# Attention and a gated MLP on one core: the first unit's gate product on ScalarE and GpSimd, and three moves in the order of work around it

## The chip, the cores and the metric

The kernel runs on one core of a Trainium2 chip. The metric is the device time of one execution in microseconds (us); lower is better. The time before is the median of three runs, 710.67 us (710.22 to 710.93).

## The reference

Causal attention over 4 batches, 12 heads, 448 positions and head size 64, then a gated MLP over the 1792 tokens, all in fp32:

```python
scores = scale * np.matmul(q, k.transpose(0, 1, 3, 2))
scores = np.where(mask, -1000000000.0, scores)
...
attn = attn / (np.sum(attn, axis=-1, keepdims=True) + 1e-09)
x = (attn @ v).transpose(0, 2, 1, 3).reshape(B * S, H * D)      # 1792 x 768
gate = 1.0 / (1.0 + np.exp(-(x @ w_gate)))                      # 768 x 1536
val = x @ w_val
return (gate * val @ w_out).astype(np.float32)                  # 1536 x 768
```

## The kernel before

The work is cut by batch. Attention of a batch handles six pairs of heads; the MLP of a batch is a "unit" of 36 weight pieces (24 for gate and value, 12 for the output), each 128x768 and each used by 18 matmuls of 448 columns. Attention of batch 0 runs alone: this is the **opening**. Then unit 0 runs interleaved with attention of batch 1, unit 1 with batch 2, unit 2 with batch 3, and unit 3 alone. The stretch of unit 0 with batch 1 is called **the first unit** below.

*Attention, batches 0 and 1.* For each pair, TensorE (PE) makes scores in four blocks of 112 rows (tile `s`, L266); VectorE (DVE) masks and takes the minimum (L279, tiles `sm`, `mn`); ScalarE (ACT) takes the exponential (L283); DVE makes the reciprocal of the sums (`r`, L290 and L291); GpSimd (POOL) scales the eight blocks with it (L302); PE transposes them in five groups of four (`trans`, tile `t` of two buffers, L315); each group is copied to `pt` by ACT (L324) or DVE (L326), as the table `EV` says, whose first index is the batch; PE multiplies with the values (L339, 16 matmuls, PSUM tile `m` of three buffers); ACT and DVE split the result into a high and a low part, `xh` (L347) and `xl` (L348).

*A weight piece* (`weight`, L531 on) arrives in unit 0 as 64-bit floats: SyncE's queue loads it (L542, tile `room`), ACT rescales the high words (L545, `wd`), DVE builds the fp32 word from them in three instructions (L547, L549, L552, tile `wr`), and SyncE writes it to DRAM for later units (L555). Then, in every unit, ACT makes the high part (L560, `wh`) and POOL the low part (L561, `wl = wr - wh`). Each product is three matmuls: `xh,wh`, `xl,wh` and `xh,wl`. In later units the piece comes back from DRAM and DVE has no part in it.

*The gate.* After the six steps of a gate piece ACT takes a tanh (L598, tile `sg` in `gt`). After the value piece DVE makes `(sg + 1) * value` in one instruction, one operand in SBUF and one in PSUM (L604), ACT rounds it to `gh` (L606) and POOL takes the remainder `gl` (L607). There are 12 of these in a unit.

*The order.* Every operation is first recorded in a plan with an engine, a cost and a due time (that of the PE step that needs it, less the costs in between); `order` then walks the engines in modelled time and, on each, takes the ready operation that is due first. The engines run that order strictly, each in its own queue. When PE takes up an attention step among the matmuls is set by `att_steps`: per pair four steps, and a tuple gives each of the five transpose groups its step. `plan.behind` holds the load of a weight piece back until a given pair of the opening has its reciprocal.

Of the kernel before, what the change touches and what calls it, by code (L numbers as in the profile page):

```python
# [11 lines left out]
ACTF = mybir.ActivationFunctionType  # L12
ALU = mybir.AluOpType
PSUM = bass.MemoryType.PSUM

B, H, S, D = 4, 12, 448, 64
# [10 lines left out]
HP = H // 2  # L27
# [1 line left out]
LAG = 1  # L29
WIDE = 2  # L30
WC = 512
EV = ((2, 3), (0, 1, 2, 3, 4), (1, 3, 4), (1, 3, 4))
BUFS = dict(w64=3, wd=2, wr=3, ws=3, sm=4, raw=3, pt=3, gt=5, vr=2, st=3)
LAT, LOOK, SLACK = 0.17, 0.06, 0.2

# [148 lines left out]
def kernel(  # L184
# [7 lines left out]
    nc = tc.nc  # L192
    plan = Plan()
# [8 lines left out]
    dve = lambda n: 0.065 + n / 960  # L202
    act = lambda n, psum=0, acc=0: n / 1200 + (0.05 if psum else 0.093) + 0.093 * acc
# [4 lines left out]
    pairs = [dict(b=n // HP, k=n % HP) for n in range(B * HP)]  # L208
# [276 lines left out]
    def att_steps(b):  # L485

        L = []
        for m in range(HP + LAG + 1):
            n, c, d = (b * HP + e if 0 <= e < HP else None for e in (m, m - LAG, m - LAG - 1))
            if n is not None:  # L490
                L.append((0, lambda due, n=n: load(n)))
            if c is not None:
                L.append((0, lambda due, c=c: load_v(c)))
            if b >= WIDE:
                if c is not None:
                    L.append((0, lambda due, c=c: shift(c)))
                one, two = [], []
                if n is not None:
                    for bl, tag in ((0, 1), "s"), ((2,), "t"):
                        one.append((sum(keys(i) / 600 for i in bl) + 0.2, lambda due, n=n, bl=bl, tag=tag: wscore(n, bl, tag, due)))  # L500
                if d is not None:
                    two.append((2.0, lambda due, d=d: wpv(d, due)))
                if n is not None:
                    two.append((0.9, lambda due, n=n: wscore(n, (3,), "s", due)))
                for mine in (one, two):
                    if mine:
                        L.append((sum(w for w, _ in mine), lambda due, mine=mine: together(due, *(f for _, f in mine)), 1.0))
                    else:
                        L.append((0, lambda due: None, 1.0))
                continue  # L510
            steps = []
            if d is not None:
                steps.append((0 if b == 0 else 2, 2.2, lambda due, d=d: pv(d, due)))
            for e in range(5):
                if n is not None and e < 3:
                    bl = ((0, 1), (2,), (3,))[e]
                    steps.append(((0, 1, 2)[e], qk_cost(bl), lambda due, n=n, bl=bl: score(n, bl, due)))
                if c is not None:
                    steps.append(((1, 1, 2, 2, 3)[e], 0.41, lambda due, c=c, e=e: trans(c, e, due)))
            if b == 0:  # L520
                for _, w, f in steps:
                    L.append((w, lambda due, f=f: together(due, f)))
                continue
            for g in range(4):
                mine = [(w, f) for o, w, f in steps if o == g]
                if mine:
                    L.append((sum(w for w, _ in mine), lambda due, mine=mine: together(due, *(f for _, f in mine))))
        return L


    def weight(p):  # L531

        t = new("wr", [128, KD, 128], F32, BUFS["wr"])
        wd = wdram[p % NP]
        if p < NP:
            q = part(2 * DM, BUFS["w64"], p)
            words = lambda: q.t.bitcast(I32).rearrange("p (n t) -> p n t", t=2)
            d = new("wd", [128, KD * 128], I32, BUFS["wd"])
            lo, hi = (lambda: words()[:, :, 0]), (lambda: words()[:, :, 1])
            ri = lambda: t.t.rearrange("p k m -> p (k m)").bitcast(I32)  # L540
            n = KD * 128
            o = plan.op("SP", dma(128 * n * 8), lambda: nc.sync.dma_start(  # L542
                out=q.t.bitcast(I32), in_=wp[p]), [], [(q,)], extra=2.0)
            plan.behind(o, pairs[(1, 2, HP - 1)[min(p, 2)]]["r"].ops[0])
            plan.op("ACT", act(n) + 0.1, lambda: nc.scalar.activation(  # L545
                out=d.t.bitcast(F32), in_=hi().bitcast(F32), func=ACTF.Copy, scale=REBIAS), [(q,)], [(d,)])
            plan.op("DVE", 0.95, lambda: nc.vector.tensor_single_scalar(  # L547
                out=ri(), in_=d.t, scalar=3, op=ALU.logical_shift_left), [(d,)], [(t,)])
            plan.op("DVE", 1.3, lambda: nc.vector.scalar_tensor_tensor(  # L549
                out=ri(), in0=lo(), scalar=29, in1=ri(), op0=ALU.logical_shift_right, op1=ALU.bitwise_or),  # L550
                [(q,)], [(t,)])
            plan.op("DVE", 1.4, lambda: nc.vector.scalar_tensor_tensor(  # L552
                out=ri(), in0=d.t, scalar=-0x80000000, in1=ri(), op0=ALU.bitwise_and, op1=ALU.bitwise_or),
                [(d,)], [(t,)])
            plan.op("SP", dma(128 * n * 4), lambda: nc.sync.dma_start(out=wd.t, in_=t.t), [(t,)], [(wd,)], extra=2.0)  # L555
        else:
            plan.op("SP", dma(128 * KD * 128 * 4), lambda: nc.sync.dma_start(out=t.t, in_=wd.t), [(wd,)], [(t,)], extra=2.0)
        hi_ = new("wh", [128, KD, 128], F32R, BUFS["ws"])
        lo_ = new("wl", [128, KD, 128], F32R, BUFS["ws"])
        plan.op("ACT", act(768), lambda: nc.scalar.copy(hi_.t, t.t), [(t,)], [(hi_,)])  # L560
        plan.op("PL", 2.0, lambda: nc.gpsimd.tensor_tensor(  # L561
            out=lo_.t, in0=t.t, in1=hi_.t.bitcast(F32), op=ALU.subtract), [(t,), (hi_,)], [(lo_,)])
        return hi_, lo_


    def unit_items(u):
# [15 lines left out]
        def f_in(jj, gv, k, due):  # L582
# [8 lines left out]
            ps = st["ps"]  # L591
# [4 lines left out]
            if gv == 0:  # L596
                st["sg"] = sg = new("gt", [128, S], F32, BUFS["gt"])
                plan.op("ACT", act(S, 1), lambda: nc.scalar.activation(  # L598
                    out=sg.t, in_=ps.t[:, :S], func=ACTF.Tanh, scale=0.5), [(ps,)], [(sg,)])
                return  # L600
            sg = st["sg"]
            gg = new("gt", [128, S], F32, BUFS["gt"])
            gh, gl = st["gh"][jj], st["gl"]
            plan.op("DVE", dve(S), lambda: nc.vector.scalar_tensor_tensor(  # L604
                out=gg.t, in0=sg.t, scalar=1.0, in1=ps.t[:, :S], op0=ALU.add, op1=ALU.mult), [(sg,), (ps,)], [(gg,)])
            plan.op("ACT", act(S), lambda: nc.scalar.copy(gh.t, gg.t), [(gg,)], [(gh,)])  # L606
            plan.op("PL", 1.3, lambda: nc.gpsimd.tensor_tensor(  # L607
                out=gl.t[:, jj], in0=gg.t, in1=gh.t.bitcast(F32), op=ALU.subtract), [(gg,), (gh,)], [(gl, jj)])
# [108 lines left out]
```

## Time and profile before

| | |
|---|---|
| median of 3 runs | 710.67 us |
| the profiled execution | 710.71 us |
| its span, first to last instruction | 709.0 us |
| PE busy in the span | 686.1 us (97%) |
| POOL, ACT, DVE busy | 429.1, 335.5, 331.0 us |

The profile is of one execution. Its span lies 1.7 us under the execution's own time. Busy time is by engine; an instruction that waits for a resource after it has begun counts as busy, so a mean duration well over that of the same instruction elsewhere is a wait inside it. PE matmuls are pipelined, and each row's time covers its own pipeline, so rows overlap. "Idle before" is the time in which an engine did nothing before an instruction, with what released it. PEclk is the granted TensorE clock, 1.00 at 2.4 GHz and 0.50 at 1.2 GHz.

### The profile page before, as it was taken

How to read it: one execution, taken by the hardware profiler on the slowest of the kernel's cores; microseconds unless marked ns; L12 is line 12 of the kernel's file. 1: busy time of each engine (PE TensorE's matmuls, PEld its weight loads, DVE VectorE, ACT ScalarE, POOL GpSimd, SP SyncE). 2: the span in 40 equal slices, each digit the busy share in tenths (PEclk: the TensorE clock that was granted, in tenths of full speed). 3: DMA queues.
4: the chain of work that ended last, by engine and by line, in shares of the span. 5: the costliest groups of instructions: out<-in, count | busy, mean ns of one | idle time of the engine just before them, and what ended most of it. 6: DMA issues, size and time to landing. Idle time of an engine off the chain costs nothing.

```text
span 709.0 us, 11071 instructions
## 1 busy us (share of the span) xinstructions
PE 686.1 (97%) x3888; PEld 573.3 (81%) x3888; DVE 331.0 (47%) x778; ACT 335.5 (47%) x727; POOL 429.1 (61%) x388
## 2 busy tenths in 40 slices
PE   7899999989998999999999999999999999999997
PEld 4446778677776888888889988888889999999997
DVE  4869999999997334344450034444450000101000
ACT  6766666574564345553542255553452233333321
POOL 3553774775865467666774467667764456666652
PEclk9989999999999999999999999999999999999999
DMA  5438667576686535546566435555455433333341
GB/s 203 150 104 300 224 227 268 203 279 192 247 275 246 207 120 172 161 142 190 146 207 182 165 115 169 147 165 163 146 161 174 138 116 112 111 111 101 114 138 40
DMA packets 45559, 121.06 MB, mean 171 GB/s; under 512 B 7104, under 2 KB 10176, under 8 KB 45504
## 3 DMA queue, kind: packets, MB, share of 16 engines
q1 hardware_dynamic: 45504, 120.35, 53.0%
q8 instruction: 31, 0.51, 0.3%
q14 instruction: 24, 0.20, 0.1%
HBM read 88.08 MB, written 19.66 MB: 152 GB/s over the span
## 4 chain that ended last, share of the span: by engine, by line
PE 69%; POOL 0%; ACT 0%; issue 0%
PE m L577 61%; PE m L460 3%; PE s L381 3%; PE t L381 1%; PE m L339 1%; POOL wl L561 0%; PE t L315 0%; POOL sm L302 0%; ACT gt L622 0%
## 5 line engine op out<-in xcount | busy, mean ns | idle before, releaser
L561 POOL TENSOR_TENSOR wl<-wr,wh 128x768 fp32r<-128x768 f32 x144 | 272.4, 1893 | 225.9 <-ACT wh L560 216.3
L560 ACT CAST wh<-wr 128x768 fp32r<-128x768 f32 x144 | 120.3, 836 | 218.7 <-PE m L577 98.0
L577 PE MATMUL m<-xh,wh 128*128 128x448 f32 x576 | 215.1, 373 | 1.8 <-DVE xl L348 1.8
L577 PE MATMUL m<-xh,wl 128*128 128x448 f32 x576 | 210.6, 366 | 1.1 <-POOL wl L561 1.1
L577 PE MATMUL m<-xl,wh 128*128 128x448 f32 x576 | 210.5, 365 | 0.0
L577 PEld LDWEIGHTS m<-xh,wh 128*128 128x128 f32 x576 | 108.3, 188 | 26.8 <-issue 14.3
L577 PEld LDWEIGHTS m<-xh,wl 128*128 128x128 f32 x576 | 108.2, 188 | 10.5 <-POOL wl L561 1.4
L577 PEld LDWEIGHTS m<-xl,wh 128*128 128x128 f32 x576 | 108.3, 188 | 8.1
L577 PE MATMUL m<-gh,wl 128*128 128x448 f32 x288 | 106.1, 368 | 1.4 <-POOL wl L561 1.4
L577 PE MATMUL m<-gh,wh 128*128 128x448 f32 x288 | 106.9, 371 | 0.0
L577 PE MATMUL m<-gl,wh 128*128 128x448 f32 x288 | 105.6, 367 | 0.0
L604 DVE SCALAR_TENSOR_TENSOR gt<-gt,m 128x448 f32<-128x448 f32 x48 | 29.6, 617 | 128.9 <-PE m L577 107.0
L302 POOL TENSOR_SCALAR sm<-sm,r 112x112 f32<-112x112 f32 (+1 forms) x92 | 57.2, 644 | 26.7 <-DVE mn L279 15.1
L402 ACT ACTIVATE sm<-sm,mn 128x128 f32<-128x128 f32 (+3 forms) x84 | 43.9, 524 | 40.1 <-DVE mn L396 40.1
L607 POOL TENSOR_TENSOR gl<-gt,gh 128x448 fp32r<-128x448 f32 x48 | 58.3, 1214 | 5.2 <-ACT gh L606 5.2
L577 PEld LDWEIGHTS m<-gh,wl 128*128 128x128 f32 x288 | 54.5, 189 | 6.5 <-POOL wl L561 2.2
L577 PEld LDWEIGHTS m<-gh,wh 128*128 128x128 f32 x288 | 54.6, 189 | 6.0 <-issue 1.4
L283 ACT ACTIVATE sm<-sm,mn 112x112 f32<-112x112 f32 (+2 forms) x96 | 49.9, 521 | 18.7 <-DVE mn L279 18.2
L577 PEld LDWEIGHTS m<-gl,wh 128*128 128x128 f32 x288 | 54.5, 189 | 4.2
L552 DVE SCALAR_TENSOR_TENSOR wr<-wd,wr 128x768 int32<-128x768 int32 x36 | 56.9, 1581 | 0.6
L396 DVE CUSTOM_DVE_ANT_0 sm<-s,mask 128x128 f32<-128x128 f32 (+1 forms) x72 | 29.5, 442 | 56.9 <-PE s L381 56.5
L434 DVE STREAM_TRANSPOSE room<-sm 128x384 f32<-128x384 f32 (+2 forms) x84 | 35.2, 446 | 33.3 <-POOL sm L417 25.9
(45 smaller groups left out, 676.4 us busy)
## 6 DMA issues: line engine op xcount, KB each, us to landing
wr<-wdram SPq DMA_DIRECT2D x108, 384.0 KB, 3.2
room<-in_wp_dram SPq DMA_DIRECT2D x36, 768.0 KB, 5.3
wdram<-wr SPq DMA_DIRECT2D x36, 384.0 KB, 4.8
pt<-room SPq DMA_DIRECT2D x192, 64.0 KB, 2.6
raw<-in_qkt_dram SPq DMA_DIRECT2D x24, 448.0 KB, 4.3
vr<-in_vt_dram SPq DMA_DIRECT2D x24, 256.0 KB, 3.6
out_dram<-gt SPq DMA_DIRECT2D x24, 224.0 KB, 1.9
```

Source lines behind the costliest of these rows:

```text
L283: plan.op("ACT", act(ne, 0, 2), lambda z=z, sm=sm, i=i, ne=ne, off=off: nc.scalar.activation(out=sm.t[:QB, off:off + ne], in_=sm.t[:QB, of ...
L302: plan.op("PL", 0.35 + w / 1100, lambda args=args: nc.gpsimd.tensor_scalar(**args()), [(r_,)], [(sm, a)])
L381: nc.tensor.matmul(out=sp[z].t[place(z, i), o:o + ne], lhsT=r.t[h, s0:s0 + rows(i)], rhs=r.t[h, S:S + ne])
L396: plan.op("DVE", dve(ne) + 0.16, lambda z=z, y=y, sm=sm, i=i, o=o, ne=ne, off=off, s0=s0, at=at: nc.vector.tensor_tensor_reduce(out=sm.t[a ...
L402: plan.op("ACT", act(ne, 0, 2), lambda z=z, sm=sm, i=i, ne=ne, off=off: nc.scalar.activation(out=sm.t[:, off:off + ne], in_=sm.t[:, off:of ...
L434: plan.op("DVE", dve(128 * c) + 0.1, lambda sm=sm, i=i, o=o, c=c, at=at: nc.vector.transpose(out=tv()[:, :, at:at + 32 * c].rearrange("p r ...
L552: plan.op("DVE", 1.4, lambda: nc.vector.scalar_tensor_tensor(out=ri(), in0=d.t, scalar=-0x80000000, in1=ri(), op0=ALU.bitwise_and, op1=ALU ...
L560: plan.op("ACT", act(768), lambda: nc.scalar.copy(hi_.t, t.t), [(t,)], [(hi_,)])
L561: plan.op("PL", 2.0, lambda: nc.gpsimd.tensor_tensor(out=lo_.t, in0=t.t, in1=hi_.t.bitcast(F32), op=ALU.subtract), [(t,), (hi_,)], [(lo_,)])
L577: nc.tensor.matmul(out=ps.t[:, :S], lhsT=a.t[:, k, :], rhs=b.t if isinstance(b, Buf) else b(), start=(first and z == 0), stop=(last and z ...
L604: plan.op("DVE", dve(S), lambda: nc.vector.scalar_tensor_tensor(out=gg.t, in0=sg.t, scalar=1.0, in1=ps.t[:, :S], op0=ALU.add, op1=ALU.mult ...
L607: plan.op("PL", 1.3, lambda: nc.gpsimd.tensor_tensor(out=gl.t[:, jj], in0=gg.t, in1=gh.t.bitcast(F32), op=ALU.subtract), [(gg,), (gh,)], [ ...
```

## The change

Four edits. (1) In unit 0 the gate product leaves DVE: ACT adds 1 to the tanh (L601), ACT copies the value out of PSUM (L608), POOL multiplies the two in SBUF (L609). Units 1 to 3 keep the DVE form. (2) In the opening, three of the five transpose groups of each pair are copied by ACT instead of two. (3) The load of the third weight piece waits for the reciprocal of pair 4, no longer for that of pair 5, so it is unpacked within the opening. (4) In batch 1, the second and the fourth transpose group of each pair stand one step later.

```diff
-EV = ((2, 3), (0, 1, 2, 3, 4), (1, 3, 4), (1, 3, 4))
+EV = ((1, 2, 3), (0, 1, 2, 3, 4), (1, 3, 4), (1, 3, 4))
...
-                    steps.append(((1, 1, 2, 2, 3)[e], 0.41, lambda due, c=c, e=e: trans(c, e, due)))
+                    steps.append((((1, 1, 2, 2, 3) if b == 0 else (1, 2, 2, 3, 3))[e], 0.41, lambda due, c=c, e=e: trans(c, e, due)))
...
-            plan.behind(o, pairs[(1, 2, HP - 1)[min(p, 2)]]["r"].ops[0])
+            plan.behind(o, pairs[(1, 2, 4, HP - 1)[min(p, 3)]]["r"].ops[0])
...
                     out=sg.t, in_=ps.t[:, :S], func=ACTF.Tanh, scale=0.5), [(ps,)], [(sg,)])
+                if u == 0:
+                    plan.op("ACT", act(S), lambda: nc.scalar.activation(
+                        out=sg.t, in_=sg.t, func=ACTF.Copy, bias=1.0), [], [(sg,)])
                 return
...
-            plan.op("DVE", dve(S), lambda: nc.vector.scalar_tensor_tensor(
-                out=gg.t, in0=sg.t, scalar=1.0, in1=ps.t[:, :S], op0=ALU.add, op1=ALU.mult), [(sg,), (ps,)], [(gg,)])
+            if u == 0:
+                plan.op("ACT", act(S, 1), lambda: nc.scalar.copy(gg.t, ps.t[:, :S]), [(ps,)], [(gg,)])
+                plan.op("PL", 1.3, lambda: nc.gpsimd.tensor_tensor(
+                    out=gg.t, in0=sg.t, in1=gg.t, op=ALU.mult), [(sg,)], [(gg,)])
+            else:
+                plan.op("DVE", dve(S), lambda: nc.vector.scalar_tensor_tensor(
+                    out=gg.t, in0=sg.t, scalar=1.0, in1=ps.t[:, :S], op0=ALU.add, op1=ALU.mult), [(sg,), (ps,)], [(gg,)])
```

Below the gate the line numbers of the changed kernel are higher: the rounding to `gh` is L614, the remainder `gl` L615, the output L630 and L632.

*VectorE in the opening*, at the second weight piece (L547 and L549 unpack it, L326 is a transpose copy, L290 and L291 make the reciprocal). Before:

```order
L279 ISA sm,mn<-s,mask 112x448
L279 ISA mn 112x1
L547 TENSOR_SCALAR wr<-wd 128x768
L326 COPY pt<-t 112x448
L290 TENSOR_SCALAR r<-sum 112x8
L291 RECIPROCAL r<-r 112x8
L549 SCALAR_TENSOR_TENSOR wr<-room,wr 128x768
```

Now:

```order
L279 ISA sm,mn<-s,mask 112x448
L279 ISA mn 112x1
L547 TENSOR_SCALAR wr<-wd 128x768
L290 TENSOR_SCALAR r<-sum 112x8
L291 RECIPROCAL r<-r 112x8
L549 SCALAR_TENSOR_TENSOR wr<-room,wr 128x768
```

The copy behind L547 has gone to ScalarE, where it is the first of three in a row behind the exponentials of the same pair.

*GpSimd in the first unit*, from the scaling of batch 1's second pair to that of its third (`wl` is the low part of a weight piece, `gl` that of the gate product, `sm` the scaled scores). Before:

```order
L561 TENSOR_TENSOR wl<-wr,wh 128x768 x2
L607 TENSOR_TENSOR gl<-gt,gh_1245 128x448
L607 TENSOR_TENSOR gl<-gt,gh_1347 128x448
L561 TENSOR_TENSOR wl<-wr,wh 128x768 x3
L607 TENSOR_TENSOR gl<-gt,gh_1454 128x448
L302 TENSOR_SCALAR sm<-sm,r 112x112
L302 TENSOR_SCALAR sm<-sm,r 112x224
L302 TENSOR_SCALAR sm<-sm,r 112x336
L302 TENSOR_SCALAR sm<-sm,r 112x448
```

Now:

```order
L561 TENSOR_TENSOR wl<-wr,wh 128x768 x2
L609 TENSOR_TENSOR gt<-gt 128x448 x2
L561 TENSOR_TENSOR wl<-wr,wh 128x768
L615 TENSOR_TENSOR gl<-gt,gh_1350 128x448
L615 TENSOR_TENSOR gl<-gt,gh_1354 128x448
L561 TENSOR_TENSOR wl<-wr,wh 128x768
L302 TENSOR_SCALAR sm<-sm,r 112x112
L302 TENSOR_SCALAR sm<-sm,r 112x224
L302 TENSOR_SCALAR sm<-sm,r 112x336
L561 TENSOR_TENSOR wl<-wr,wh 128x768
L302 TENSOR_SCALAR sm<-sm,r 112x448
```

Two products (L609) stand in the queue between weight pieces, and weight pieces now also stand between the scalings, of which all eight ran in a row before.

*TensorE in the first unit*, at the third step of a pair of batch 1 (L339 is the product with the values, L266 the scores of the next pair's last block, L315 the transposes). Before:

```order
L339 MATMUL m<-pt,vr 64x448 x2
L339 MATMUL m<-pt,vr 64x336 x2
L339 MATMUL m<-pt,vr 64x224 x2
L339 MATMUL m<-pt,vr 64x112 x2
L266 MATMUL s<-raw 112x448 x2
L315 MATMUL t<-ident,sm 112x112 x8
```

Now:

```order
L339 MATMUL m<-pt,vr 64x448 x2
L339 MATMUL m<-pt,vr 64x336 x2
L339 MATMUL m<-pt,vr 64x224 x2
L339 MATMUL m<-pt,vr 64x112 x2
L315 MATMUL t<-ident,sm 112x112 x4
L266 MATMUL s<-raw 112x448 x2
L315 MATMUL t<-ident,sm 112x112 x4
```

The group ahead of the scores is the second one, which stood a step earlier; the fourth has left for the step behind. In the opening, PE's order is as it was but for one transpose group.

## Rows read from the trace of the kernel before

**Rows 1.** Busy time by stretch: opening, first unit, the rest; then PEclk, DMA share, GB/s

```profile
0.00:63.00 63.00, 54.28 (x325) 30.38 (x326) 44.43 (x155) 42.97 (x129) 27.68 (x54) 0.95 0.52 175
63.00:218.00 155.00, 144.49 (x764) 114.13 (x764) 147.24 (x200) 95.94 (x204) 108.22 (x88) 1.00 0.71 247
218.00:704.00 486.00, 486.00 (x2797) 427.86 (x2796) 139.28 (x425) 196.02 (x395) 293.15 (x247) 1.00 0.48 147
```

**Rows 2.** Groups of instructions by form, 0 to 60 us, PE's transposes with their idle time

```profile
L315 PE MATMUL t<-ident,sm 112*112 112x112 f32 x116 | 15.7, 272 | 3.6 <-DVE pt L326 2.6 <-ACT pt L324 0.7 <-POOL sm L302 0.3
```

**Rows 3.** Timeline of PE, DVE and POOL around the opening's longest wait

```profile
34.11 0.98 PE L315 MATMUL t<-ident,sm 112*112 112x112 f32 x8 [1.46 <-DVE pt L326]
...
31.85 1.67 DVE L547 TENSOR_SCALAR wr<-wd 128x768 int32<-128x768 int32 x1
...
31.29 1.81 POOL L561 TENSOR_TENSOR wl<-wr,wh 128x768 fp32r<-128x768 f32 x1
```

**Rows 4.** Busy time by 10 us, columns as in Rows 1: the slower clock

```profile
30.00:40.00 10.00, 8.16 (x42) 4.40 (x42) 9.04 (x26) 6.76 (x20) 7.42 (x12) 0.81 0.36 105
40.00:50.00 10.00, 10.00 (x64) 5.07 (x60) 5.01 (x22) 6.89 (x21) 3.55 (x5) 0.85 0.37 113
```

**Rows 5.** Groups by form, 0 to 60 us: DVE's copies and weight unpacking, ACT's copies

```profile
L326 DVE COPY pt<-t 112x448 f32<-112x448 f32 x17 | 10.5, 618 | 3.3 <-PE t L315 3.3
L324 ACT COPY pt<-t 112x448 f32<-112x448 f32 x12 | 6.3, 530 | 5.9 <-PE t L315 5.9
...
L549 DVE SCALAR_TENSOR_TENSOR wr<-room,wr 128x768 int32<-128x768 int32 x3 | 2.8, 933 | 0.0
L547 DVE TENSOR_SCALAR wr<-wd 128x768 int32<-128x768 int32 x3 | 2.8, 925 | 0.0
...
L552 DVE SCALAR_TENSOR_TENSOR wr<-wd,wr 128x768 int32<-128x768 int32 x2 | 2.0, 1002 | 0.0
```

**Rows 6.** Waits of PE in the first unit, 63 to 218 us: total, times, longest

```profile
PE t L315 <- POOL sm L302: 4.6, 10, 1.0
PE m L577 <- POOL wl L561: 2.5, 3, 1.1
PE m L577 <- DVE xl L348: 1.8, 2, 0.9
PE s L266 <- DVE mn L279: 0.9, 2, 0.5
PE m L339 <- DVE gt L604: 0.6, 1, 0.6
```

**Rows 7.** Groups by form, 63 to 218 us, DVE

```profile
L552 DVE SCALAR_TENSOR_TENSOR wr<-wd,wr 128x768 int32<-128x768 int32 x28 | 48.1, 1716 | 0.5
L549 DVE SCALAR_TENSOR_TENSOR wr<-room,wr 128x768 int32<-128x768 int32 x28 | 39.3, 1404 | 0.5
L547 DVE TENSOR_SCALAR wr<-wd 128x768 int32<-128x768 int32 x29 | 37.2, 1284 | 3.6 <-POOL wl L561 3.6
L604 DVE SCALAR_TENSOR_TENSOR gt<-gt,m 128x448 f32<-128x448 f32 x12 | 7.3, 607 | 0.0
```

**Rows 8.** Groups by form, POOL: 63 to 218 us, and below 250 to 560 us

```profile
L561 POOL TENSOR_TENSOR wl<-wr,wh 128x768 fp32r<-128x768 f32 x28 | 58.4, 2090 | 45.3 <-ACT wh L560 45.3
L607 POOL TENSOR_TENSOR gl<-gt,gh 128x448 fp32r<-128x448 f32 x12 | 16.8, 1398 | 5.2 <-ACT gh L606 5.2
...
L607 POOL TENSOR_TENSOR gl<-gt,gh 128x448 fp32r<-128x448 f32 x24 | 27.6, 1150 | 0.0
```

**Rows 9.** Timeline in the first unit: one unpacking instruction on DVE, and POOL beside it

```profile
156.03 5.81 DVE L549 SCALAR_TENSOR_TENSOR wr<-room,wr 128x768 int32<-128x768 int32 x1
...
157.39 3.63 POOL L561 TENSOR_TENSOR wl<-wr,wh 128x768 fp32r<-128x768 f32 x2
```

**Rows 10.** Chain of work that ended last (start, us, what): the first pieces behind the first unit

```profile
217.44 3.68 PE m L577 x10
...
224.06 7.31 PE m L577 x36
```

## The prediction

> **What bounds the kernel now.** The busy time by stretch comes first [rows 1]. PE is busy for all of the 486 us from 218 to 704 us: whatever is gained or lost before 218 us moves the end by as much. In the opening PE is busy 54.3 of 63 us, of which 3.9 us is the wait for the first load, so 4.8 us is idle. In the first unit it is busy 144.5 of 155 us, so 10.5 us is idle. DVE is busy 147.2 of those 155 us and POOL only 108.2, which makes DVE look like the bound there.
>
> Then who releases PE. In the opening 2.6 of 3.6 us at the transposes wait for DVE's copies out of PSUM [rows 2]; the longest wait, 1.46 us, ends when a copy ends that was queued behind an unpacking instruction [rows 3]. In the first unit [rows 6] five causes add up to 10.4 us: 4.6 us for POOL's scaling, 2.5 us for POOL's low parts, and 1.8, 0.9 and 0.6 us for DVE's `xl`, minima and gate product.
>
> Third, why DVE is full. An unpacked piece takes 0.933 + 0.925 + 1.002 = 2.86 us of DVE in the opening [rows 5], and 1.716 + 1.404 + 1.284 = 4.40 us in the first unit [rows 7]. The extra 1.54 us is waiting inside the instruction: one L549 lasted 5.81 us, from 156.03 to 161.84, and POOL ran two low parts from 157.39 to 161.02 [rows 9]; in the opening an L547 took 1.67 us over a low part on POOL [rows 3]. DVE's unpacking and POOL's work get in each other's way. POOL pays as well: its 128x448 remainder takes 1.398 us in the first unit and 1.150 us later, where nothing is unpacked [rows 8].
>
> Last, the clock. PEclk is 0.81 from 30 to 40 us and 0.85 from 40 to 50 us [rows 4]: (0.19 + 0.15) x 10 = 3.4 us of clock not granted, right behind the 1.46 us wait. At 217.44 us, behind the first unit's last waits, ten matmuls take 3.68 us; 36 take 7.31 us further on [rows 10]. That is 0.37 against 0.20 us each, so 1.65 us is lost there too.
>
> **The change part by part.**
>
> *Opening, copies.* Six copies (one for each of six pairs) leave DVE: 6 x 0.618 = 3.7 us. They cost ACT 6 x 0.530 = 3.2 us [rows 5]. ACT is busy 43 of 63 us [rows 1], but three of its copies now stand in a row behind exponentials, so a transpose that waited for DVE may wait for ACT. Of the 2.6 us I take 1.5 off; the bounds are 2.6 off and, with an ACT wait as long as the one removed, none.
>
> *Opening, clock.* If the 1.46 us wait shrinks, I expect the slower clock behind it not to come. It is worth at most 3.4 us. DVE is busy only 5.0 of 10 us while PE runs slowly [rows 4], and without it DVE and ACT are the next thing that is late, so I take 2.0; the bounds are 3.4 and 0, where the clock falls elsewhere.
>
> *Opening, third piece.* Its load goes ahead of one load of values and one of queries and keys in SyncE's queue, where the DMA share is 0.37 [rows 4], which covers it. Its 2.86 us on DVE stand against 3.7 us freed there. I take 0.5 us lost; the bounds are 0 and 2.9, as if nothing covered it. The opening sums to -1.5 - 2.0 + 0.5 = -3.0 us.
>
> *First unit, DVE's side.* Twelve gate products go: 12 x 0.607 = 7.3 us; one piece goes: 4.4 us. Together 11.7 us.
>
> *First unit, POOL's side.* Twelve multiplies come. No row shows one; the nearest is the remainder, also two SBUF tensors of 128x448, at 1.150 to 1.398 us [rows 8], so 13.8 to 16.8 us. One low part of 2.09 us goes to the opening. POOL gains 11.7 to 14.7 us; I take 13.2, and POOL is then busy 121 of 155 us.
>
> *First unit, what POOL's time costs DVE.* Some 28.5 pieces lose 1.54 us each, 44 us, beside 108.2 us of busy POOL: 0.41 us of DVE for each of POOL. 13.2 us more cost 5.4 us, and DVE is relieved of 11.7 - 5.4 = 6.3 us. The bounds are 11.7 (the multiplies fall where DVE unpacks nothing) and -1.5 (each microsecond of POOL costs one of DVE).
>
> The Trainium skill, GPSIMD Engine Reference, section Key points, says that GpSimd shares its SBUF interfaces with VectorE and contends with VectorE instructions in a 2-port mode or with two SBUF inputs. The trace agrees in that L604, with one input in PSUM, takes 0.607 us in the first unit [rows 7], while the unpacking swells. By that rule the change takes an instruction off VectorE that did not contend and gives GpSimd one that does.
>
> *First unit, PE's side.* The waits for `xl`, minima and gate product are DVE operations late by at most 0.9 us at a time [rows 6]. A relief of 6.3 us spread over the stretch covers them: -3.3 us. The PSUM tile that L604 freed is now freed by ACT's copy L608; ACT is busy 96 of 155 us [rows 1] and gains 24 instructions of about 0.53 us, 13 us, so it stays at 70%. Of the 7.1 us on POOL, the moved transposes take something off: two of five groups per pair ask for their scaled scores a quarter of a pair's time later. But the first group stays, and there a low part now stands between the scalings. I take 2.5 off for the moved groups and the earlier reciprocals, and 1.5 on for POOL's longer queue: -1.0; the bounds are -7.1 and +2.8 (the waits grow by two fifths). The moved transposes themselves cost nothing, since PE does as many, and their copies have until the next product with the values. The first unit sums to -4.3 us. The slow clock at 217 us is left as it is in the sum.
>
> *Units 1 to 3* keep their form and their full PE: 0.
>
> *Sum.* 710.71 (the profiled execution: its span of 709.0 and 1.7 around it) - 3.0 - 4.3 = 703.4 us. The median is 0.04 us under the profiled execution, so it stays 703.4.
>
> **The rivals.**
>
> *Most of the waits go* (A). POOL's multiplies fall into its gaps, as its 45 us of waiting for ACT [rows 8] would let them. Then the opening gives 2.6 + 3.4 - 1 = 5.0 us and the first unit 8 to 10.4 us, with the 1.65 us of clock behind it: about 14 us, 696.5. Against it: the first transpose group still asks for its scores as early as before.
>
> *The first unit gives nothing* (B). DVE's relief is used up by POOL's longer queue: the 3.3 us of DVE waits go, and as much comes at the low parts, for which PE already waited three times [rows 6]. The opening's 3 us remain: 707.7 us.
>
> *The shared way into SBUF becomes the bound* (C), slower. The first unit needs DVE's unpacking and POOL's work one after the other. If each added microsecond of POOL costs DVE more than 11.7 / 13.2 = 0.89 us, DVE has less room than before. At one for one the stretch is 1.5 us longer, POOL's waits at PE grow by 2.8 us, and the opening's clock falls a few microseconds later instead of not at all, so that the opening gives 0 to 1 us: about 714 us. For it: the 5.81 us instruction [rows 9], where DVE lost all of POOL's time. Against it: the mean price of 0.41. By the Trainium skill's rule above, this rival is the one to fear, and the trace bears it out in part.
>
> *The edits do not move what they name* (D): the copies on ACT come too late to shorten the opening's wait, and the plan sets the new operations so that all engines run as late as before. 710 us, no difference.
>
> **How the numbers follow.** The forecast (699.5 to 707) has 0.48, A 0.15, B 0.17, C 0.14, D 0.06. A measurement of this kernel tells 0.2%, 1.4 us, from no change, so faster is under 709.25 and slower over 712.1. The forecast, A and nearly all of B are faster: 0.79. D and a little of B and C are the same: 0.08. Slower, from C, is 0.13. The predicted time is that of the forecast, 703.4 us. The range leaves out the lower half of A and nearly all of C: 696.5 to 710.5 us.
>
> **What would show it.** Right: PE's wait at the opening's transposes falls under 2 us, PEclk stays at 1.00 from 30 to 50 us, a piece of DVE's unpacking in the first unit takes 4.4 to 4.8 us, DVE's busy time there falls by about 6 us, and PE's waits sum to some 6 us, nearly all on POOL. Wrong: an unpacked piece takes 5 us or more (C), PE waits for `wl` as long as for `sm` (B), or the clock falls again in the opening (forecast too fast by 2 us). It would also be wrong if POOL's multiply took well over 1.4 us, or if PE showed waits for ACT's copies.

## The result, and the profile after

The changed kernel takes **719.51 us**, the median of five runs (719.25 to 720.85), against 710.67 us for the kernel before (709.13 to 712.49, also five). The ratio is 1.014, with a 95% interval of 1.0121 to 1.0159: slower, where 703.4 us was forecast. The profiled execution took 720.85 us, its span is 719.1 us.

Two rows of PE's timeline bound the first unit: the first matmul of its first weight piece, and that of unit 1's first piece. Before, then after:

```profile
62.80 0.47 PE L577 MATMUL m<-xh,wh 128*128 128x448 f32 x1
...
253.30 0.36 PE L577 MATMUL m<-xh,wh 128*128 128x448 f32 x1
```

```profile
61.69 0.47 PE L577 MATMUL m<-xh,wh 128*128 128x448 f32 x1
...
263.41 0.37 PE L577 MATMUL m<-xh,wh 128*128 128x448 f32 x1
```

The opening became 1.1 us shorter and the first unit 11.2 us longer (201.7 against 190.5 us). Together that is the 10.1 us by which the spans differ; units 1 to 3 are as they were (455.7 us in both). Of the two, the first unit's share is the certain one: three runs below keep the changed kernel's order (c1, h2 and h2b), and in them the same opening ends at 61.70 to 63.34 us, with the clock low for 3 to 7 us of it. The stretches of [rows 1] after the change, in its columns:

```profile
0.00:63.00 63.00, 54.38 (x330) 30.98 (x331) 44.22 (x153) 47.24 (x140) 30.57 (x55) 0.97 0.56 189
63.00:218.00 155.00, 140.88 (x716) 111.48 (x715) 143.16 (x177) 98.67 (x212) 115.03 (x89) 0.94 0.66 223
```

In the first unit DVE is busy 143.16 us against 147.24 before, and PE waits longer for DVE all the same. PE's waits there, which answer to [rows 6]:

```profile
PE s L266 <- DVE mn L279: 10.2, 3, 5.9
PE t L315 <- POOL sm L302: 2.0, 4, 0.9
PE m L577 <- DVE xl L348: 1.9, 1, 1.9
```

The waits for `wl` and for the gate product are gone, those for the scaling are more than halved. In their place are three waits for the minima. From 218 us to the end of the unit, 2.6 us more go to ACT's copies of the transposes:

```profile
PE t L315 <- ACT pt L324: 1.6, 1, 1.6
PE m L339 <- ACT pt L324: 1.0, 1, 1.0
```

That is 16.7 us where 10.4 us were.

What the engines did around the longest of the three, in the timelines of PE, DVE and POOL (start, length, idle before):

```profile
162.81 0.82 PE L266 MATMUL s<-raw 64*112 64x336 f32 x2
...
169.56 1.46 PE L266 MATMUL s<-raw 64*112 64x336 f32 x2 [5.93 <-DVE mn L279]
...
160.76 0.96 DVE L549 SCALAR_TENSOR_TENSOR wr<-room,wr 128x768 int32<-128x768 int32 x1
161.76 1.09 DVE L552 SCALAR_TENSOR_TENSOR wr<-wd,wr 128x768 int32<-128x768 int32 x1
162.77 0.55 DVE L547 TENSOR_SCALAR wr<-wd 128x768 int32<-128x768 int32 x1
163.35 5.65 DVE L549 SCALAR_TENSOR_TENSOR wr<-room,wr 128x768 int32<-128x768 int32 x1
168.93 0.26 DVE L279 CUSTOM_DVE_ANT_0 sm<-s,mask 112x112 f32<-112x112 f32 x1
...
159.42 4.84 POOL L302 TENSOR_SCALAR sm<-sm,r 112x112 f32<-112x112 f32 x4
164.22 1.79 POOL L561 TENSOR_TENSOR wl<-wr,wh 128x768 fp32r<-128x768 f32 x1
165.98 1.12 POOL L615 TENSOR_TENSOR gl<-gt,gh 128x448 fp32r<-128x448 f32 x1
167.07 1.12 POOL L609 TENSOR_TENSOR gt<-gt 128x448 f32<-128x448 f32 x1
```

PE has made two blocks of scores and needs their minima before it can make the next. The minima stand in DVE's queue behind an L549. That instruction takes 0.96 us three rows further up, while POOL scales; begun at 163.35 us it lasts 5.65 us, through `wl`, `gl` and the new product (L609), which follow each other on POOL without a gap. It ends 0.8 us after the product does. Before the change there was an instruction just as long [rows 9]. There the four minima had been made in the 1.0 us ahead of it, the last at 155.72 us, and PE's scores of that pair did not wait (before, DVE and PE):

```profile
155.72 0.38 DVE L279 CUSTOM_DVE_ANT_0 sm<-s,mask 112x224 f32<-112x224 f32 x1
...
156.22 0.82 PE L266 MATMUL s<-raw 64*112 64x336 f32 x4
```

So the length of the hold-up is not new. In the first unit six unpacking instructions last over 2.9 us before and eight after, the longest 5.81 and 5.79 us. What stands behind them on DVE is new.

The wait of 4.09 us has no product in it: it ends at 132.91 us, and the first two L609 beside it begin on POOL at 132.83 us. There the minima stand behind the unpacking of two pieces, of which one L547 lasts 4.12 us (from 121.98 us) over scalings and a low part.

The second loss is the clock. Busy time by 10 us, columns as above:

```profile
30.00:40.00 10.00, 8.81 (x57) 4.92 (x57) 9.44 (x26) 7.95 (x23) 7.32 (x12) 1.00 0.39 111
...
50.00:60.00 10.00, 8.29 (x50) 4.80 (x52) 6.85 (x20) 5.52 (x13) 3.22 (x5) 0.83 0.82 307
...
130.00:140.00 10.00, 7.09 (x20) 5.41 (x20) 9.90 (x16) 5.86 (x16) 7.95 (x7) 0.66 0.51 183
...
160.00:170.00 10.00, 4.07 (x19) 3.10 (x19) 9.90 (x15) 4.96 (x11) 8.19 (x7) 0.80 0.59 203
170.00:180.00 10.00, 10.00 (x42) 7.02 (x43) 6.91 (x12) 7.05 (x19) 5.44 (x4) 0.69 0.75 238
```

In the first unit the clock is at its lower level, 1.2 GHz, from 131.8 us, near the end of a wait of 4.09 us for the minima, and from 166.0 us, within the wait of 5.93 us. The last three rows miss 3.4 + 2.0 + 3.1 = 8.5 us of clock, which is 17.0 us at half. PE stood idle for 4.7 us of those, so some (17.0 - 4.7) / 2 = 6.2 us are lost (an estimate), 4.5 us more than the 1.65 us before. With 6.3 us more of waits this gives 10.8 of the 11.2 us. In the opening the clock now stays at 1.00 from 30 to 50 us. It falls at 53 us instead of 36 us and is low for 3.4 us instead of 6.8, beside a wait of PE's transposes for POOL:

```profile
53.30 0.96 PE L315 MATMUL t<-ident,sm 112*112 112x112 f32 x4 [1.38 <-POOL sm L302]
```

Third, what DVE and POOL pay each other, which answers to [rows 7, 8] (groups by form, 63 to 218 us):

```profile
L549 DVE SCALAR_TENSOR_TENSOR wr<-room,wr 128x768 int32<-128x768 int32 x26 | 46.6, 1792 | 0.7
L552 DVE SCALAR_TENSOR_TENSOR wr<-wd,wr 128x768 int32<-128x768 int32 x26 | 40.6, 1561 | 0.6
L547 DVE TENSOR_SCALAR wr<-wd 128x768 int32<-128x768 int32 x26 | 34.8, 1338 | 5.7 <-POOL wl L561 5.7
...
L615 POOL TENSOR_TENSOR gl<-gt,gh 128x448 fp32r<-128x448 f32 x12 | 17.1, 1435 | 3.1 <-ACT gh L614 3.1
L609 POOL TENSOR_TENSOR gt<-gt 128x448 f32<-128x448 f32 x12 | 17.0, 1422 | 11.8 <-DVE mn L279 6.0 <-ACT gt L608 5.7
```

A piece takes 1.792 + 1.561 + 1.338 = 4.69 us of DVE, 0.29 us more than before.

### The profile page after: what moved, and what is told of

It reads as the page before. It is cut to its first block, busy times and chain, and to the rows that moved or that the text cites. A ratio compares the mean times of both kernels' runs of the same rounds, so it can differ in the third digit from the quotient of the medians.

```text
span 719.1 us, 11057 instructions
## 1 busy us (share of the span) xinstructions
PE 690.0 (96%) x3888; PEld 576.7 (80%) x3888; DVE 331.2 (46%) x760; ACT 349.0 (49%) x757; POOL 449.6 (63%) x400
## 4 chain that ended last, share of the span: by engine, by line
PE 67%; ACT 1%; DMA 1%; issue 1%; SPq 0%; ACTq 0%
PE m L577 59%; PE m L460 3%; PE s L381 3%; PE t L381 1%; DMA room<-in_wp_dram 1%; ACT wh L560 0%; PE m L339 0%; ACT gt L630 0%; PE t L315 0%; ACT wd L545 0%; ACT pt L324 0%; ACT sm L283 0%; SPq L632 0%; ACTq L545 0%; SPq L542 0%
## 5 line engine op out<-in xcount | busy, mean ns | idle before, releaser
L561 POOL TENSOR_TENSOR wl<-wr,wh 128x768 fp32r<-128x768 f32 x144 | 272.1, 1890 | 208.9 <-ACT wh L560 199.2
L560 ACT CAST wh<-wr 128x768 fp32r<-128x768 f32 x144 | 120.4, 836 | 196.5 <-PE m L577 102.3
L612 DVE SCALAR_TENSOR_TENSOR gt<-gt,m 128x448 f32<-128x448 f32 x36 | 22.3, 620 | 129.0 <-PE m L577 106.7
L302 POOL TENSOR_SCALAR sm<-sm,r 112x112 f32<-112x112 f32 (+1 forms) x92 | 61.6, 688 | 23.0 <-DVE mn L279 15.5
L283 ACT ACTIVATE sm<-sm,mn 112x112 f32<-112x112 f32 (+3 forms) x96 | 50.0, 523 | 28.5 <-DVE mn L279 27.8
L615 POOL TENSOR_TENSOR gl<-gt,gh 128x448 fp32r<-128x448 f32 x48 | 58.5, 1221 | 3.1 <-ACT gh L614 3.1
L549 DVE SCALAR_TENSOR_TENSOR wr<-room,wr 128x768 int32<-128x768 int32 x36 | 58.4, 1623 | 0.9
L266 PE MATMUL s<-raw 64*112 64x112 f32 (+3 forms) x192 | 43.9, 463 | 15.5 <-DVE mn L279 11.4
```

Source lines behind the costliest of these rows:

```text
L266: nc.tensor.matmul(out=sp[z].t[:QB, o:o + ne], lhsT=r.t[h, s0:s0 + QB], rhs=r.t[h, S:S + ne])
L283: plan.op("ACT", act(ne, 0, 2), lambda z=z, sm=sm, i=i, ne=ne, off=off: nc.scalar.activation(out=sm.t[:QB, off:off + ne], in_=sm.t[:QB, of ...
L302: plan.op("PL", 0.35 + w / 1100, lambda args=args: nc.gpsimd.tensor_scalar(**args()), [(r_,)], [(sm, a)])
L549: plan.op("DVE", 1.3, lambda: nc.vector.scalar_tensor_tensor(out=ri(), in0=lo(), scalar=29, in1=ri(), op0=ALU.logical_shift_right, op1=ALU ...
L561: plan.op("PL", 2.0, lambda: nc.gpsimd.tensor_tensor(out=lo_.t, in0=t.t, in1=hi_.t.bitcast(F32), op=ALU.subtract), [(t,), (hi_,)], [(lo_,)])
L615: plan.op("PL", 1.3, lambda: nc.gpsimd.tensor_tensor(out=gl.t[:, jj], in0=gg.t, in1=gh.t.bitcast(F32), op=ALU.subtract), [(gg,), (gh,)], [ ...
```

## The experiments

The theory after the result, called P in the expectations: POOL's products hold DVE's unpacking up while both work on operands in SBUF, the held-up unpacking delays what stands behind it on DVE, PE waits, and its clock falls. The rivals: E, the changed order of DVE's, PE's and POOL's queues and ACT's new copies do the harm, not the product; O, the other edits do. Ratios are against the kernel before on the same chip; the kernel before took 709.02 to 710.67 us on these chips, so a difference in us between runs of two chips is good to some 1.6 us. "First unit" is the stretch between the two rows at the top (190.5 us before, 201.7 after). An edit that changes an engine, a cost or a due time makes the plan order all engines anew; only c1, h2 and h2b keep the changed kernel's order.

**Each edit alone**, on the kernel before. The product, as in the diff of the change (cut here; ACT's addition goes with it):

```diff
+            if u == 0:
+                plan.op("ACT", act(S, 1), lambda: nc.scalar.copy(gg.t, ps.t[:, :S]), [(ps,)], [(gg,)])
+                plan.op("PL", 1.3, lambda: nc.gpsimd.tensor_tensor(
```

> The gate product alone goes to ScalarE and GpSimd; copies, third piece and transposes stay as before. Theory P (GpSimd's added tensor-tensor work holds up VectorE's unpacking, so the minima come late and TensorE waits for its score buffers): 716 to 722 us, with one or two waits of 3 us or more for the minima in the first unit. Theory O (the moved transposes and the order that follows from them make the minima late): 706 to 711 us. Theory S (the third piece and the copies shift the first unit's start): 706 to 711 us.

718.68 us, ratio 1.0134 (1.0096 to 1.0173); first unit 198.3 us. PE's waits from 63 to 218 us:

```profile
PE m L577 <- DVE xl L348: 7.3, 3, 4.1
PE m L577 <- POOL wl L561: 3.0, 2, 1.8
PE s L266 <- DVE mn L279: 1.2, 1, 1.2
PE t L315 <- POOL sm L302: 0.7, 3, 0.3
```

The time came out as P said, the place did not: long waits for the minima were expected, and here DVE's late operation is `xl`. The product alone is enough for nearly all the harm. That the other edits do none does not follow; b1 below tests it. A piece takes 4.65 us.

The three copies, the third piece and the moved transposes, each alone:

```diff
-EV = ((2, 3), (0, 1, 2, 3, 4), (1, 3, 4), (1, 3, 4))
+EV = ((1, 2, 3), (0, 1, 2, 3, 4), (1, 3, 4), (1, 3, 4))
```

> Only the opening's copies, three of five on ScalarE. All theories: a gain of about 1 to 3.5 us (707 to 710 us), the wait of 1.46 us at the transposes shorter and the slow clock behind it gone; the first unit as before. If the slow clock only moves, 710 us.

706.97 us, ratio 0.996 (0.9941 to 0.998). The opening ends 2.5 us earlier, at 60.34 us; its clock still falls once, for half as long (3.5 us). The edit is good by itself.

```diff
-            plan.behind(o, pairs[(1, 2, HP - 1)[min(p, 2)]]["r"].ops[0])
+            plan.behind(o, pairs[(1, 2, 4, HP - 1)[min(p, 3)]]["r"].ops[0])
```

> Only the third weight piece unpacked in the opening. P and O: 706 to 711 us, since VectorE has one piece less in the first unit and pays 2.9 us in the opening. S: slower, 713 us or more.

709.83 us, ratio 0.9999 (0.9976 to 1.0022): nothing. The opening's one fall of the clock comes at 51.7 instead of 36.2 us and again lasts 6.8 us.

```diff
-                    steps.append(((1, 1, 2, 2, 3)[e], 0.41, ...
+                    steps.append((((1, 1, 2, 2, 3) if b == 0 else (1, 2, 2, 3, 3))[e], 0.41, ...
```

> Only the second and fourth transpose group of batch 1 a step later. O: 715 us or more, with long waits for the minima. P and S: 708 to 711 us, the waits for the scaled scores down by 1 to 3 us.

710.0 us, ratio 1.0007 (0.9989 to 1.0026): nothing in sum. The waits for the scaling did shrink, and one wait of 4.30 us for a copy on ACT took their place. The timelines of PE and ACT show why:

```profile
214.65 0.97 PE L315 MATMUL t<-ident,sm 112*112 112x112 f32 x4 [4.30 <-ACT pt L324]
...
212.41 0.83 ACT L560 CAST wh<-wr 128x768 fp32r<-128x768 f32 x1 [5.23 <-DVE wr L552]
```

The copy stood behind a cast (L560) that waited 5.23 us for a piece that DVE was still unpacking.

**The changed kernel without the product's work.** Every instruction in its place, the product cut from 448 columns to 4, which leaves 444 columns of it out:

```diff
-                    out=gg.t, in0=sg.t, in1=gg.t, op=ALU.mult), [(sg,)], [(gg,)])
+                    out=gg.t[:, :4], in0=sg.t[:, :4], in1=gg.t[:, :4], op=ALU.mult), [(sg,)], [(gg,)])
```

> The changed kernel with every instruction in its place, but each of the twelve GpSimd multiplies works on 4 of 448 columns, so the gate product is left out; ScalarE's two extra instructions stay. P (the multiply's time on GpSimd, in the way of VectorE's unpacking): 703 to 711 us, most of the 9 us comes back, and an unpacked piece takes less than in the changed kernel. Q (the order the plan makes once the product leaves VectorE, with unpacking ahead of minima and low parts between scalings): 715 us or more, waits for the minima as long as in the changed kernel. R (ScalarE's longer queue): 715 us or more, with waits on ScalarE.

709.01 us, ratio 1.0007 (0.9966 to 1.0048); first unit 189.4 us, a piece 4.30 us. POOL's row for it:

```profile
L609 POOL TENSOR_TENSOR gt<-gt 128x4 f32<-128x4 f32 x12 | 5.7, 480 | 9.2 <-ACT gt L608 9.2
```

12 x (1.422 - 0.480) = 11.3 us of POOL's work, whose spans are rough, were worth 719.5 - 709.0 = 10.5 us of the end (9.4 us by the two ratios), not far from one for one, with every queue in the same order. The ten times spread from 706.24 to 716.46 us, and the longest is still below the changed kernel's shortest, 719.25. So in this order it is the product's time on POOL that costs, as P says, and ACT's 24 new instructions, which stay, do not by themselves make the kernel slower than before. Nor is it the product's own lateness: PE in the changed kernel never waits for the product or its remainder, and ACT's rounding waits 0.6 us in all for L609. The order keeps a share, so E is not out: two waits for the minima, of 4.1 and 2.7 us, remain, and the kernel only draws level although DVE has been spared its 7.3 us of products.

**The changed kernel with DVE's form of the product** (edits 2 to 4 alone), and with every second product on POOL:

```diff
-            if u == 0:
+            if u < 0:
```

> Copies, third piece and transposes as changed; the gate product as before. P, Q and R: 704 to 709 us, near the copies alone, since the product alone took the 9 us. If the edits work against each other: 712 us or more.

716.14 us, ratio 1.0084 (1.0058 to 1.0111). A miss: three edits that singly give -3.6, -0.8 and -0.6 us (the last two can't be told from nothing) cost 6.2 us together, 5.9 us of it in the first unit (196.4 us). So O holds for the three together: without any product on POOL they cost two thirds of what the change costs. The two harms do not add, since 8.1 us (a1) and 6.2 us come to 8.8 us in the changed kernel. The largest wait is again for ACT's copy, in PE's timeline:

```profile
220.73 0.97 PE L315 MATMUL t<-ident,sm 112*112 112x112 f32 x4 [6.14 <-ACT pt L324]
```

```diff
-            if u == 0:
+            if u == 0 and jj % 2 == 0:
```

> The changed kernel with the product on ScalarE and GpSimd for every second of the twelve. P: halfway, 711 to 716 us, GpSimd's added time being half. Q: as slow as the changed kernel or near the kernel without it, as the order falls, not halfway. R: halfway as well.

714.68 us, ratio 1.0081 (1.0048 to 1.0115): with half the products some 4 to 5 us of the 8.8 us come back. The order was planned anew and has b1's collision beneath it, so this run alone would not separate P from E.

**Which edits collide.** The copies with the third piece, and the copies with the moved transposes, both without the product (the first one's edit is shown; the second has the line of the moved transposes in place of the last):

```diff
+EV = ((1, 2, 3), (0, 1, 2, 3, 4), (1, 3, 4), (1, 3, 4))
+            plan.behind(o, pairs[(1, 2, 4, HP - 1)[min(p, 3)]]["r"].ops[0])
```

> Copies and third piece, transposes and product as before. The three edits without the product were 6 us slower than the kernel before while each alone was not; this pair tells which. X (copies and piece collide at the end of the opening, where the third piece delays the last pair's scaling): 711 us or more, PE's first weight piece at 62 us or later and the clock slow behind it. Y (the collision needs the moved transposes): 705 to 709 us.

> Copies and moved transposes, piece and product as before. X: 705 to 709 us. Y (the moved transposes make PE ask for the next pair's scores before VectorE has done the minima, and for a transpose buffer before ScalarE has copied it): 711 us or more, with waits for the minima near 130 and 160 us.

713.29 us, ratio 1.007 (1.0028 to 1.0113), and 708.14 us, ratio 0.9993 (0.997 to 1.0016). With the third piece the opening has the changed kernel's fault, in PE's timeline:

```profile
53.27 0.74 PE L315 MATMUL t<-ident,sm 112*112 112x112 f32 x4 [1.26 <-POOL sm L302]
```

The clock is low there from 53.5 to 56.9 us. The copies alone show neither. In f1 the last pair's four scalings on POOL take 3.10 us, with an L549 of the third piece beside them on DVE; with the copies alone they take 2.07 us. But this is the smaller part: f1's opening ends at 61.67 us, 1.3 us behind the copies alone, and its first unit takes 194.1 us against 189.0, with a wait of 3.3 us for the minima. It has one piece less to unpack and is longer; why stays open.

**The minima first.** In the changed kernel, batch 1's minima are given the due time of their scores, so that they go ahead of unpacking:

```diff
-                ), [(sp[z],), (mask,)], [(sm, i), (mn, (z, i))])
+                ), [(sp[z],), (mask,)], [(sm, i), (mn, (z, i))], due if j["b"] == 1 else None)
```

> The changed kernel, with the due time of batch 1's minima set to that of their scores, so that the plan puts them ahead of the unpacking. P with its last link (unpacking that waits for GpSimd stands ahead of the minima, and PE's score buffers wait for those): the waits of 4 and 6 us for the minima go, and of the 9 us some 5 to 8 come back: 711 to 715 us; the unpacked piece still takes as long as in the changed kernel. If the minima are late for another reason (ScalarE, PE's order): 718 us or more.

720.82 us, ratio 1.0188 (1.015 to 1.0227): a miss, P expected 711 to 715. The waits for the minima fell from 10.2 to under 4 us, and those for `xl` rose (PE's waits, 63 to 222 us):

```profile
PE m L577 <- DVE xl L348: 10.2, 2, 6.6
PE s L266 <- DVE mn L279: 3.4, 3, 2.6
```

The loss does not belong to the minima. As in a1, it went to another operation of DVE that was due while unpacking was held up. The order was planned anew here too.

**Less on POOL.** The kernel before with edit 2, and unit 0's remainder `gl` moved from POOL to DVE:

```diff
+EV = ((1, 2, 3), (0, 1, 2, 3, 4), (1, 3, 4), (1, 3, 4))
...
-            plan.op("PL", 1.3, lambda: nc.gpsimd.tensor_tensor(
+            e, cost_, eng = ("DVE", dve(S) + 0.05, nc.vector) if u == 0 else ("PL", 1.3, nc.gpsimd)
+            plan.op(e, cost_, lambda: eng.tensor_tensor(
```

> The kernel before with the opening's copies as changed, and in unit 0 the remainder gl moved from GpSimd to VectorE: the opposite direction. P: the same two-SBUF operation is about half as long on VectorE, so the time in which the two engines exclude each other shrinks: 702 to 707 us. If VectorE's own busy time is the bound of the first unit: 710 us or more, since 7 us of work comes to it.

**699.13 us, ratio 0.983 (0.979 to 0.9871): faster than both kernels.** Groups by form and PE's waits, 63 to 218 us:

```profile
L552 DVE SCALAR_TENSOR_TENSOR wr<-wd,wr 128x768 int32<-128x768 int32 x30 | 42.0, 1399 | 0.5
L549 DVE SCALAR_TENSOR_TENSOR wr<-room,wr 128x768 int32<-128x768 int32 x30 | 39.7, 1324 | 0.4
L547 DVE TENSOR_SCALAR wr<-wd 128x768 int32<-128x768 int32 x30 | 36.5, 1217 | 1.0 <-POOL sm L302 0.6 <-ACT wd L545 0.4
...
L608 DVE TENSOR_TENSOR gl<-gt,gh 128x448 fp32r<-128x448 f32 x12 | 12.9, 1081 | 0.0
```

```profile
PE m L577 <- POOL wl L561: 2.8, 3, 1.2
PE s L266 <- DVE mn L279: 1.1, 1, 1.1
PE t L315 <- POOL sm L302: 0.8, 3, 0.3
```

DVE takes on 12 x 1.081 = 13.0 us and a piece falls to 3.94 us, 0.46 us less for each of 30, or 13.8 us: the busiest engine of the first unit, DVE, was given more work and is busy no longer for it. The first unit takes 180.5 us against 189.0 with edit 2 alone, its waits are 4.7 us, and PEclk is 1.00 in both stretches. That is better than P's range. The order was planned anew, so how much of it the order gives is not shown.

Further the same way, with every low part `wl` of unit 0 on DVE too, and with every second one:

```diff
-        plan.op("PL", 2.0, lambda: nc.gpsimd.tensor_tensor(
+        e, c_, eng = ("DVE", 1.0, nc.vector) if p < NP else ("PL", 2.0, nc.gpsimd)
+        plan.op(e, c_, lambda: eng.tensor_tensor(
```

> Copies as changed, unit 0's remainder and all 36 low parts of unit 0 on VectorE, the product as before: GpSimd keeps the scaling alone. P: an unpacked piece falls towards 2.9 us, and VectorE's 36 low parts of about 1 us are paid by that: 694 to 701 us. If VectorE's work is the bound: 706 us or more.

> As the run with all low parts on VectorE, but for every second piece. P: between that one and the remainder alone (699 us), 694 to 700 us.

701.71 us, ratio 0.9883 (0.9843 to 0.9922), and 705.84 us, ratio 0.9946 (0.9921 to 0.9972). Both miss P's ranges, the first by 0.7 us. The first is also the measurement of the disputed cost, since POOL has only the scalings left in the first unit (groups by form, 63 to 218 us):

```profile
L549 DVE SCALAR_TENSOR_TENSOR wr<-room,wr 128x768 int32<-128x768 int32 x28 | 27.7, 990 | 0.2
L562 DVE TENSOR_TENSOR wl<-wr,wh 128x768 fp32r<-128x768 f32 x28 | 26.9, 962 | 17.9 <-ACT wh L560 17.9
L552 DVE SCALAR_TENSOR_TENSOR wr<-wd,wr 128x768 int32<-128x768 int32 x27 | 26.4, 977 | 0.4
...
L547 DVE TENSOR_SCALAR wr<-wd 128x768 int32<-128x768 int32 x28 | 16.6, 593 | 0.0
```

A piece takes 0.990 + 0.977 + 0.593 = 2.56 us, so POOL's work with two operands in SBUF is what costs DVE 1.84 us a piece in the kernel before. It is no better than the version above, though: PE now waits 6.4 us for the scaling, in 10 waits, and POOL's scalings take 0.933 us on average where they took 0.749 us before. The half measure is worse than either, with 4.4 us of waits for the scaling and 3.7 us for `wl`; a piece takes 3.20 us there. So the price of a piece does not by itself set the end: 3.94 us of it end at 699 us, 3.20 at 706 and 2.56 at 702.

**The changed kernel with one of POOL's two gate instructions on DVE.** First planned anew with the remainder there (the edit of the 699.13 us version), then with the recorded order kept and the product or the remainder run by DVE (the remainder's edit is shown):

```diff
-            plan.op("PL", 1.3, lambda: nc.gpsimd.tensor_tensor(
+            plan.op("PL", 1.3, lambda: (nc.vector if u == 0 else nc.gpsimd).tensor_tensor(
```

> The changed kernel, with unit 0's remainder gl on VectorE, so that GpSimd has as many tensor-tensor operations as in the kernel before (the multiply in place of the remainder). P: 703 to 711 us, the 9 us come back. If the product's longer chain over two engines is the cost, not GpSimd's time: 716 us or more.

> The changed kernel with every instruction at its place in the one recorded order, but unit 0's multiply run by VectorE in that place (still two SBUF tensors), so that GpSimd has none of it. P (the time in which GpSimd's and VectorE's two-input work exclude each other sets the loss; the multiply is shorter on VectorE): 706 to 714 us, between the kernel with 4 columns and the changed one. If it is enough that VectorE has more to do than before: 719 us or more.

> The changed kernel in its recorded order, with the multiply on GpSimd and unit 0's remainder run by VectorE in its old place. The version that the planner ordered anew gave nothing back (720.5 us). P with the order as a second cause: 708 to 716 us here. If P is wrong and the longer chain over the engines is the cost: 719 us or more, as there.

| run | median, us | ratio (95%) | a piece, us |
|---|---|---|---|
| remainder, planned anew | 720.5 | 1.0176 (1.0139 to 1.0213) | 4.28 |
| product, same order | 714.79 | 1.007 (1.0043 to 1.0098) | 4.13 |
| remainder, same order | 716.25 | 1.0089 (1.0058 to 1.012) | 4.16 |

In the same order a piece gets cheaper and 4.7 and 3.3 us come back, the side that P names, though both times lie just over its ranges (714 and 716 us). Planned anew the piece gets cheaper too and nothing comes back, a miss. The trace says where it goes. In the profiled execution, the slowest of four, the first unit takes 198.8 us, 2.9 us less than in the changed kernel, though the waits for the minima are 11.0 us, the longest 7.2 us. The opening takes 67.4 us, 5.7 us more, with the clock low from 36.7 to 43.6 and from 57.2 to 64.0 us:

```profile
0.00:63.00 63.00, 55.09 (x296) 30.74 (x296) 39.60 (x144) 43.43 (x128) 28.70 (x54) 0.90 0.54 185
```

A new order can take away, in another stretch, what POOL's shorter work gives back.

## Why the prediction was wrong

*Opening, copies* (-1.5): right for the edit by itself, which brought the opening forward by 2.5 us with the clock's share. In the changed kernel the wait for DVE's copies [rows 2] is gone, but 1.3 us for ACT's copies and 2.0 us for the scaling stand in its place, so PE's waits at the transposes fell from 3.6 to 3.3 us only.

```profile
L315 PE MATMUL t<-ident,sm 112*112 112x112 f32 x120 | 16.7, 274 | 3.3 <-POOL sm L302 2.0 <-ACT pt L324 1.3
```

*Opening, clock* (-2.0) and *third piece* (+0.5): the fall at 36 us went, and one at 53 us came, beside a wait that the copies with the third piece show too (f1) and the copies alone do not. The text named this as a way to be wrong ("the clock falls again in the opening") and put the price at 2 us; the opening gave 1.1 us instead of 3.0, which is 1.9. That the price fits so well is in part luck, since the same opening ends up to 1.65 us apart in four executions.

*First unit, DVE's side and POOL's side*: the instructions cost about what was said (the product 1.422 us, a little over the 1.15 to 1.40 taken).

*What POOL's time costs DVE* (5.4 us): a piece rose by 0.29 us, 8.1 us over 28 pieces, for the 15.0 us that POOL gained (12 x 1.422 less a low part of 2.09). That is 0.54 us for each of POOL against 0.41. The term was too small, but DVE is still relieved, by 3.6 us instead of 6.3, so rival C's condition, 0.89, was not reached.

*First unit, PE's side* (-4.3): **this is the step that failed**, with its sentence that "a relief of 6.3 us spread over the stretch covers them". DVE did get some relief, and PE's waits for DVE went from 3.3 to 12.1 us. A mean says nothing of a wait: PE waits where an operation that is due stands behind unpacking that is held up. The three waits for the minima, 10.2 us, show it; in a1 and f3 it is `xl` that stands there. The part for POOL's waits (-1.0) had the right side and was too small: 4.6 and 2.5 us became 2.0 and none, which is -5.1 us. And the sentence that the moved transposes "cost nothing" did not hold: PE waits 2.6 us for ACT's copies of transposes, where it waited for none before, and 4.30 us with the moved transposes alone (a4).

*The slow clock "is left as it is in the sum"*: the second half of the error. Beside the long waits the clock was at its lower level for 17 us, which by the estimate above lost 4.5 us more than before. The four parts, +8.8 for DVE, -5.1 for POOL, +2.6 for the copies and +4.5 for the clock, come to the 10.8 us above.

So the first unit gave +11.2 instead of -4.3 us, the opening -1.1 instead of -3.0, and 15.5 + 1.9 = 17.4 us is what separates the profiled execution of 720.85 us from 703.4 us.

*The rivals.* C had the side and the mechanism: POOL's work with two operands in SBUF holds up DVE's unpacking. c1, h2 and h2b show in one order that this work costs time, and h1 shows its price for a piece; e1 gains as P says, with an order of its own. Its place was wrong, since it expected POOL's waits at PE to grow, and its 714 us lacked the waits for DVE and the clock behind them. The rule of the Trainium skill, GPSIMD Engine Reference, section Key points, on VectorE instructions with two SBUF inputs, agrees with L549 and L552 (1.792 and 1.561 us in the changed kernel, 0.990 and 0.977 us when POOL only scales). A, B and D are out.

*Left open:* how much of the 11.2 us another order of the same work would save (c1 leaves waits of 6.9 us for the minima with no product to speak of); why edits 2 to 4 cost 6.2 us together without the product, most of it in the first unit, and why the copies with the third piece alone already lengthen that unit; and how the planner came to f4's opening.

## What to carry to other kernels

Before work is moved to GpSimd because it looks idle, see whether VectorE beside it runs instructions that swell when GpSimd works: here instructions with two operands in SBUF, moved onto GpSimd, were paid nearly one for one at the end, and the opposite move, from GpSimd to the busier VectorE, came with a gain of some 7 us over edit 2 alone (10.8 against 3.6 us, each on its chip). Price a contended engine by what stands in its queue behind the held-up instructions, not by its mean busy time: the longest of them lasted 5.8 us before and after, and only after did PE wait long for what stood behind. Allow for the clock too, which was low for 17 us beside two such waits. Edits that gain or do nothing singly can cost together, so time them together and undo each.

## What the runs showed of the hardware

- VectorE got its turn among GpSimd's scalings (L549 0.96 and L552 1.09 us at 160.76 and 161.76 us, beside four L302 that took 4.84 us), but one L549 lasted 5.65 us, over three tensor-by-tensor instructions that followed each other there. It is not always so: the L549 of the kernel before [rows 9] ended at 161.84 us, in the middle of a third such instruction (L607, 160.97 to 162.84 us).
- An instruction with a single operand is held up too: L547 takes 0.52 us at its shortest, 1.338 us on average in the changed kernel, and 0.593 us on average when GpSimd only scales.
- GpSimd pays in turn: its scalings take 0.749 us on average in the first unit before, and 0.933 us when VectorE makes all the low parts and remainders.
- The same subtraction of 128x768 takes 0.962 us on VectorE (L562) and 1.79 us on GpSimd (L561 at 164.22 us).
- TensorE's clock fell to its lower level beside single waits of 1.38 us (changed kernel) and 1.26 us (f1) in the opening, and for 6.8 and 10.2 us beside waits of 4.09 and 5.93 us.
